# Leftover columns of a row transform as 32-row products with split frequency tables, and 64 small products ahead of the first column product

## Chip, cores, metric

The kernel runs on one core of one Trainium2 chip. The metric is the device time of one execution in microseconds. Three runs of the kernel before gave 494.93, 494.39 and 494.04 us, median 494.39 us.

## What is computed

```python
def _A_ref(x, w_r, w_i):                       # x: 1 x 2048 x 576
    X = rfft2(x.astype(float32), axes=(-2, -1))
    X = X * (w_r + 1j * w_i)
    return irfft2(X, s=(S, D)).astype(bfloat16)

def _B_ref(x, w_gate, w_up, w_down):           # 576 -> 4608 -> 576
    return (_gelu(x @ w_gate) * (x @ w_up)) @ w_down

h  = x + _A_ref(_layernorm(x), A_w_r, A_w_i)
h2 = h + _B_ref(_layernorm(h), B_w_gate, B_w_up, B_w_down)
```

x has 2048 rows of 576 values in bfloat16. The first part is a layer norm, a two-dimensional Fourier transform, a product with a filter and the transform back. The second part is a gated feed-forward network. The change lies in the forward transform.

## The kernel before, in words

The 2048 rows lie as 128 partitions by H = 16 (`h_sb`, partition p and index h hold row 16p + h). Every transform is a matrix product on TensorE with tables of sines and cosines that the kernel makes itself. The order on each engine is the order of the program text (a manual schedule); nothing is reordered between engines, and a wait on an engine holds all that is behind it on that engine.

The head of the kernel goes like this.

- **Statistics.** For most h VectorE takes mean and variance (`sd`, lines 379 to 387); for h = 1, 3, 5, 9, 11 ScalarE does (`ln_act`, line 128). GpSimd turns variances into reciprocal deviations (lines 137, 138), in the groups 0 to 3, 4 to 7, 8 to 11, 12 and 13, 14 and 15, and also issues two gathers of filter rows (line 397).
- **Tables.** ScalarE makes a table `fs` (line 218) by a sine, VectorE makes `F16` of it (`row_table`, line 298), and `small_table` (line 429) is the first use of it on TensorE. Then `fill` (line 316) gives TensorE 12 products of 512 columns whose result is not used.
- **First row step.** `norms` (line 389) scales `F16` by the reciprocal deviations into `FR` (line 391, VectorE), and `row16(h)` multiplies the 128-column blocks of row group h by it (lines 327 and 334, six products of 256, 256 and 128 columns for each half). 512 of the 576 columns are done so, in four blocks: columns 0 to 127 and 128 to 255, and the same from DH = 288 on.
- **Leftover columns.** Columns 256 to 287 and 544 to 575 are left. `row16_rest(h)` takes 64 columns from 256 and 64 from 512, so that 32 of each are needed and 32 overlap with what `row16` has; the two products write partitions 0 to 63 and 64 to 127 of one PSUM bank. Two more with `mneg` take the mean away. `rests(h)` does this for four h: 16 products of 128 columns with 64-column weights. It is called four times, after h = 3, 7, 11 and 15.
- **Evictions.** `evict` (line 361, ScalarE) copies two h at a time from PSUM into `Bt`; `evict4` (line 367) copies four h of leftovers, 128 x 512 values, on ScalarE for h = 0 and 4 and on VectorE for 8 and 12. All PSUM tiles come from one ring of four (`two`), so a new tile waits for the eviction of the fourth one before it.
- **Column step.** `f2(c)` (line 550) multiplies a 128-column slice of `Bt` by `DT` (four products of 290 columns) and `DF` (two, for the leftovers). `DF` is `D3` with the partitions of the overlapping columns set to zero. For the first c the two `DF` products stand last. `f2_out` (line 561) copies out on ScalarE. From here on the column products, the filter, the transform back and the feed-forward network follow, TensorE being busy nearly all the time.
- **Tables for the way back.** `load_dq` (line 518, DMAs on SyncE's queue) copies the rows of `DT` for frequencies into `DQ`; `iD` (lines 205 to 207) says which column each partition stands for.

Of the kernel before, what the change touches and what calls it, by code (L numbers as in the profile page):

```python
# [9 lines left out]
ACT = mybir.ActivationFunctionType  # L10
ALU = mybir.AluOpType
FP32 = mybir.dt.float32
BF16 = mybir.dt.bfloat16
# [7 lines left out]
P = 128  # L21
S = 2048
H = 16
D = 576
DH = D // 2
J = D // 2 + 1
JP = J + 1
JH = JP // 2
# [5 lines left out]
JW = 58  # L34
NW = JP // JW
# [7 lines left out]
def kernel_body(  # L43
# [11 lines left out]
    nc = tc.nc  # L55
    V = nc.vector
    A = nc.scalar
    G = nc.gpsimd
    T = nc.tensor

    ctx.enter_context(tc.manual_schedule())
    keep = ctx.enter_context(tc.tile_pool(name="keep", bufs=1))
# [4 lines left out]
    def two(name):  # L67
        return psum.tile([P, 2, 512], FP32, name=name, tag="two", bufs=4)

    h_sb = keep.tile([P, H, D], BF16, name="h_sb")  # L70
# [6 lines left out]
    def const(name, val):  # L77
        t = keep.tile([P, 1], FP32, name=name)
        V.memset(t[:], val)
        return t  # L80

    zerob = const("zerob", 0.0)
    pib = const("pib", PI)
    npib = const("npib", -PI)
    hpib = const("hpib", 0.5 * PI)
    nhpib = const("nhpib", -0.5 * PI)
# [5 lines left out]
    mneg = keep.tile([P, 2, H], BF16, name="mneg")  # L92
# [5 lines left out]
    Bt = keep.tile([P, NDT, S], BF16, name="Bt")  # L98
# [4 lines left out]
    ident = keep.tile([P, P], BF16, name="ident")  # L103
# [4 lines left out]

    DT = keep.tile([P, 3, 2, 2, JH], BF16, name="DT")
    D3 = DT[:, 2]  # L110
    DF = keep.tile([P, 2, 2, JH], BF16, name="DF")
    DQ = keep.tile([P, NW, 2, JH], BF16, name="DQ")
    mv = keep.tile([P, H, 2], FP32, name="mv")
    rstd = keep.tile([P, H], FP32, name="rstd")
# [67 lines left out]
    def tmp(name, shape, dtype=I32):  # L182
        return scr.tile(shape, dtype, name=name)

    def iota(t, pattern, base=0, cm=0):
        G.iota(t, pattern=pattern, base=base, channel_multiplier=cm, allow_small_or_imprecise_dtypes=True)

    V.memset(DF[:], 0.0)
    V.memset(DT[:, :, 1, :, JH - 1], 0.0)

    iu, ic = tmp("iu", [P, H, 8]), tmp("ic", [P, H, 8])
# [12 lines left out]
    make_identity(nc, ident[:])  # L204
    iD = tmp("iD", [P, 3], FP32)
    iota(iD[:], [[P, 3]], 0, 1)
    iota(iD[64:128, 2:3], [[0, 1]], 2 * P + 64 + 192, 1)
    iJ = tmp("iJ", [P, 2 * JM], FP32)
    iota(iJ[:], [[1, 2], [2, JM]])
    iDs = tmp("iDs", [P, 3], FP32)  # L210
# [72 lines left out]
    def minus_sine(sl):  # L283
        V.tensor_scalar(TF[:, sl, 0, :], TF[:, sl, 2, :], -1.0, None, op0=ALU.mult)
# [25 lines left out]
    ps_f = {}  # L310
# [28 lines left out]
                stop=True,  # L339
            )  # L340

    def rests(h):
        ps_f["f4", h] = two("f4")
        for i in range(4):
            row16_rest(h + i)

    def row16_rest(h):
        o = (h % 4) * P
        for mean in (False, True):
            for p0, d0 in ((0, 256), (64, 512)):  # L350
                T.matmul(
                    ps_f["f4", h - h % 4][p0 : p0 + 64, 0, o : o + P],
                    lhsT=mneg[:, 1, h : h + 1].to_broadcast([P, 64]) if mean else h_sb[:, h, d0 : d0 + 64],
                    rhs=FR[:, h, 0, :],
                    start=not mean,
                    stop=mean,
                )

    def evict(*hs):
        for h in hs:  # L360
            A.copy(  # L361
                Bt[:, 0:4, :].rearrange("p t (c h l) -> p (t c) h l", c=16, h=16)[:, :, h : h + 2, :],
                ps_f[h][:].rearrange("p h (tc l) -> p tc h l", l=8),
            )

    def evict4(h):
        (V.tensor_copy if h >= 8 else A.copy)(
            Bt[:, 4, :].rearrange("p (c h l) -> p h c l", c=16, h=16)[:, h : h + 4, :, :],
            ps_f["f4", h][:, 0].rearrange("p (h c l) -> p h c l", h=4, c=16),
        )  # L370

    agg = []
# [16 lines left out]
    def norms(lo, hi):  # L389
        for h in range(lo, hi):  # L390
            V.tensor_scalar(FR[:, h], F16[:], rstd[:, h : h + 1], None, op0=ALU.mult)  # L391
            row16(h)
# [12 lines left out]
    FR = fr_pool.__enter__().tile([P, H, 2, P], BF16, name="FR")  # L405
# [10 lines left out]
    def mirror(r):  # L416

        for a in range(2):
            dst, src, sg = DT[:, :, a, r, JM - a : JH - a], DT[:, :, a, r, JM - 2 :: -1], sgn[:, r : r + 1]
            V.tensor_scalar(dst, src, sg, None, op0=ALU.mult)  # L420
# [38 lines left out]
    minus_means(4, 8)  # L459
    gather(0)  # L460
    norms(0, 4)
    rests(0)
    minus_sine(first)
    turn_tf(first)
    sd(8, 10)
    flush()
    norms(4, 8)
    rests(4)
    ln_fin(slice(9, 12, 2))
    ln_rstd(rstd, mv, 8, 12)  # L470
    minus_means(8, 12)
    gather(1)
    evict(0, 2)
    evict4(0)
    evict(4, 6)
    evict4(4)
    sd(12, 13)
    flush()
    ln_rstd(rstd, mv, 12, 14)
    minus_means(12, 14)  # L480
    phases(0)
    norms(8, 12)
    rests(8)
    sd(14, 15)
    flush()
    ln_rstd(rstd, mv, 14, 16)
# [2 lines left out]
    phases(1, 2)  # L489
    drop_sign(kd[:], pd[:])  # L490
    norms(14, 16)
    rests(12)
    evict(8, 10)
    col_sin(1, pd, zerob)
    col_sin(0, kd, hpib)
    evict(12, 14)
    mirror(1)
    mirror(0)
    evict4(8)
    V.tensor_copy(DF[0:32], D3[0:32])  # L500
    V.tensor_copy(DF[96:128], D3[96:128])
    evict4(12)
    for w, t in ((WR, wm[0]), (WI, wm[1])):
        nc.sync.dma_start(w[:, 9 : H + 1, 0:J], t[:].rearrange("p (r j) -> p r j", r=8))
    angle_a(rest)
# [6 lines left out]
    def load_dq(r):  # L512
        for w in range(1 - r, NW):
            j0, j1 = w * JW, (w + 1) * JW
            for lo, hi in ((j0, min(j1, (j0 // P + 1) * P)), ((j0 // P + 1) * P, j1)):
                if lo < hi:
                    p0 = 64 * r + lo - j0
                    nc.sync.dma_start(
                        DQ[p0 : p0 + hi - lo, w], DT[lo % P : lo % P + hi - lo, lo // P, :, r, :]
                    )  # L520

    load_dq(1)

# [12 lines left out]
    order = [1, 2, 3, 4, 5, 6, 7, 0]  # L536
# [4 lines left out]
    slot = {k + 8 * e: 8 * x + 4 * e + i for k, (x, i) in place.items() for e in range(2)}  # L541

    def f2(c):
        ps = two("pq_ps")
        col = slice(slot[c] * P, (slot[c] + 1) * P)
        steps = [(par, t) for par in range(2) for t in (par, par + 2, 4)]
        if c == order[0]:
            steps.sort(key=lambda s: s[1] == 4)
        for par, t in steps:
            T.matmul(  # L550
                ps[:, par, 0:JP],
                lhsT=Bt[:, t, col],
                rhs=DT[:, t // 2, par] if t < 4 else DF[:, par],
                start=(t == par),
                stop=(t == 4),
            )
        pq[c] = wk.tile([P, 2, JP], BF16, name="pq", tag="pq", bufs=6)
        pq_ps[c] = ps
# [179 lines left out]
    n = len(order)  # L738
# [75 lines left out]
    def p_sb(f):  # L814
        if f >= NP0 and len(P_sb) == 1:
            P_sb.append(fp.tile([P, NFT - NP0, 4 * P], BF16, name="P_sb", tag="P1"))
        return P_sb[f // NP0][:, f % NP0, :]
# [138 lines left out]
    for h in range(4, H):  # L956
        b = 6 * (h // 2 - 2)
# [4 lines left out]
        b = h // 4 * NFT - NFT + 3 * (h % 4) + 2 + 16 * (h < 8)  # L962
# [36 lines left out]
    for tcnk in range(4):  # L999
        for gi in range(NG):  # L1000
# [7 lines left out]
            n = tcnk * NG + gi  # L1008
# [4 lines left out]
        for st in range(4):  # L1013
            h = tcnk * 4 + st
            if h < H - 1:
                accs = [two("acc") for _ in range(2)]
                for f in range(NFT):
                    for c in range(2):
                        for i in range(2):
# [3 lines left out]
                                lhsT=p_sb(f)[rows, st * P : (st + 1) * P],  # L1023
                                rhs=wd[f // NWA][rows, f % NWA, c * DH : (c + 1) * DH],
                                start=(f == 0),
                                stop=(f == NFT - 1),
# [9 lines left out]
            for c in range(2):  # L1036
                cc = slice(c * DH, (c + 1) * DH)
                acc = two("acc")
                for f in range(NFT):
                    T.matmul(  # L1040
                        acc[:, 0, 0:DH],
                        lhsT=p_sb(f)[:, st * P : (st + 1) * P],
                        rhs=wd[f // NWA][:, f % NWA, cc],
                        start=(f == 0),
                        stop=(f == NFT - 1),
# [54 lines left out]
```

## Time and profile before

| | us |
|---|---|
| median of three runs | 494.39 |
| the profiled execution, time | 494.6 |
| the profiled execution, span from first to last instruction | 492.8 |
| outside the span | 1.8 |
| TensorE busy in the span | 484.7 |
| first column product starts (after the span's start) | 21.96 |

The span is read from the left: the first 22 us are the head described above, 22 to about 65 us are the rest of the spectral part, and everything behind is the feed-forward network. All starts below are counted from the span's start. A busy TensorE is not TensorE at its peak: a product's recorded duration has a latency in it, and the distance between the starts of products tells more.

### The profile page before, as it was taken

To read this page: it belongs to the slowest core of one execution; us is meant where nothing else is said; L and a number is where in the kernel's file an instruction comes from. 1 tells how busy PE (TensorE), PEld (TensorE's weight loads), DVE (VectorE), ACT (ScalarE), POOL (GpSimd) and SP (SyncE) were. 2 spreads that over 40 slices of the span, in tenths; PEclk is the share of its full clock that TensorE was granted. 3 is DMA by queue.
4 is the path that set the end of the run, shared out by engine and by line. 5 is a ranking of instruction groups with operands and counts; after the bars stand their busy time and mean duration, and the time that the engine had idled before them with its cause. 6 is when DMAs were issued, how large, how long until landed. Compare 5 with 4: busy or idle time off the path is not lost.

```text
span 492.8 us, 12868 instructions
## 1 busy us (share of the span) xinstructions
PE 484.7 (98%) x5762; PEld 338.9 (69%) x5762; DVE 223.4 (45%) x457; ACT 158.2 (32%) x280; POOL 29.5 (6%) x84
## 2 busy tenths in 40 slices
PE   6999999999999999999999999999999999999997
PEld 3777789875589955555699755555799655555995
DVE  8999774798622177333311345333121333333111
ACT  8899863322210022332200132332110232232000
POOL 8500010011100011000000000000000000000000
PEclk9999999999999999999999999999999999999999
DMA  8838979769970049966720089876600377760000
GB/s 278 234 74 184 246 115 240 165 128 212 223 161 3 3 118 195 192 145 147 152 65 1 37 170 199 174 145 147 143 3 3 92 158 155 150 146 1 14 13 25
DMA packets 89582, 62.35 MB, mean 127 GB/s; under 512 B 23222, under 2 KB 88118, under 8 KB 89526
## 3 DMA queue, kind: packets, MB, share of 16 engines
q1 hardware_dynamic: 89238, 60.34, 57.5%
q0 software_dynamic: 288, 1.18, 0.7%
q8 instruction: 45, 0.74, 0.7%
q14 instruction: 11, 0.09, 0.1%
HBM read 52.65 MB, written 2.36 MB: 112 GB/s over the span
## 4 chain that ended last, share of the span: by engine, by line
PE 95%; ACT 2%; POOL 1%; DMA 1%; issue 0%; DVE 0%; ACTq 0%; POOLq 0%
PE gu L978 57%; PE acc L1021 27%; PE pq_ps L550 2%; PE cs_ps L709 2%; PE acc L1040 2%; PE eo_ps L658 2%; ACT junk L128 1%; PE y_ps L848 1%; PE gh_ps L568 1%; PE gh_ps L567 1%; DMA h_sb<-in_A_x_dram 1%; POOL rstd L138 1%; ACT Bt L361 0%; POOL wm_r L397 0%; PE eo_ps L682 0%
## 5 line engine op out<-in xcount | busy, mean ns | idle before, releaser
L978 PE MATMUL gu<-Bt,wgu 64*128 64x512 bf16 (+1 forms) x2646 | 270.6, 363 | 0.0
L978 PEld LDWEIGHTS <-wgu 64*128 64x128 bf16 x2646 | 151.5, 94 | 115.6 <-issue 0.3
L987 DVE TENSOR_TENSOR P_sb<-g_sb,gu 128x512 bf16<-128x512 f32 (+1 forms) x156 | 100.4, 645 | 140.3 <-ACT g_sb L986 140.3
L986 ACT ACTIVATE g_sb<-gu 128x512 f32<-128x512 f32 (+1 forms) x156 | 88.0, 564 | 193.5 <-PE gu L978 193.5
L1021 PEld LDWEIGHTS <-P_sb 64*128 64x128 bf16 x2160 | 122.2, 94 | 10.9
L1021 PE MATMUL acc<-wd,P_sb 64*128 64x288 bf16 x1440 | 90.9, 283 | 0.0
L1030 DVE TENSOR_TENSOR part<-part,acc 128x576 f32<-128x576 f32 x15 | 11.3, 754 | 112.6 <-ACT part L1029 112.6
L1029 ACT COPY part<-acc 128x576 f32<-128x576 f32 x15 | 9.6, 639 | 122.8 <-PE acc L1021 122.8
L1021 PE MATMUL acc<-wd_a,P_sb 64*128 64x288 bf16 x720 | 46.8, 283 | 0.0
L550 PE MATMUL pq_ps<-DT,Bt 128*128 128x290 bf16 x64 | 12.3, 286 | 0.7 <-ACT Bt L361 0.7
L978 PE MATMUL gu<-Bt,wgu_e 64*128 64x256 bf16 (+1 forms) x162 | 12.5, 305 | 0.0
L873 DVE TENSOR_SCALAR hrow<-h_sb,mv,rstd 128x1152 bf16<-128x1152 bf16 x14 | 12.2, 868 | 0.6 <-POOL rstd L911 0.6
L138 POOL TENSOR_TENSOR rstd<-rstd,mhalf 128x1 f32<-128x1 f32 (+2 forms) x17 | 12.0, 709 | 1.4
L1032 DVE TENSOR_TENSOR h_sb<-h_sb,part 128x576 bf16<-128x576 bf16 x15 | 11.4, 758 | 0.5
L550 PEld LDWEIGHTS <-Bt 128*128 128x128 bf16 x96 | 9.1, 97 | 3.4 <-ACT Bt L361 0.8
L978 PEld LDWEIGHTS <-wgu_e 64*128 64x128 bf16 x162 | 10.3, 94 | 1.2
L137 POOL TENSOR_SCALAR rstd<-mv 128x1 f32<-128x1 f32 (+2 forms) x17 | 4.1, 242 | 116.7 <-DVE mv L123 116.0
L561 ACT CAST pq<-pq_ps 128x580 bf16<-128x580 f32 x16 | 10.5, 666 | 1.2 <-PE pq_ps L550 1.1
L709 PE MATMUL cs_ps<-DQ,EO 58*128 58x290 bf16 x144 | 10.8, 283 | 0.0
L327 PE MATMUL f2t<-FR,h_sb 128*128 128x256 bf16 x64 | 9.2, 273 | 0.6 <-DVE FR L391 0.6
L709 PEld LDWEIGHTS <-EO 58*128 58x128 bf16 x160 | 7.8, 94 | 2.4 <-issue 0.7
L550 PE MATMUL pq_ps<-DF,Bt 128*128 128x290 bf16 x32 | 8.9, 285 | 0.0
(149 smaller groups left out, 283.9 us busy)
## 6 DMA issues: line engine op xcount, KB each, us to landing
wgu<-in_B_w_gate_dram SPq DMA_DIRECT2D x46, 432.0 KB, 5.1
wgu<-in_B_w_up_dram SPq DMA_DIRECT2D x46, 432.0 KB, 6.1
wd_a<-in_B_w_down_dram SPq DMA_DIRECT2D x1, 1728.0 KB
wd<-in_B_w_down_dram SPq DMA_DIRECT2D x1, 1728.0 KB
wd<-in_B_w_down_dram SPq DMA_DIRECT2D x6, 288.0 KB, 7.9
out_dram<-h_sb SPq DMA_DIRECT2D x3, 576.0 KB
h_sb<-in_A_x_dram SPq DMA_DIRECT2D x4, 288.0 KB, 4.3
h_sb<-in_A_x_dram SPq DMA_DIRECT2D x2, 576.0 KB
```

The source lines that it names most:

```text
L138: G.tensor_tensor(dst[:, sl], dst[:, sl], mhalf[:, sl], ALU.pow)
L550: T.matmul(ps[:, par, 0:JP], lhsT=Bt[:, t, col], rhs=DT[:, t // 2, par] if t < 4 else DF[:, par], start=(t == par), stop=(t == 4),)
L561: copy(pq[c][:, rs].rearrange("p r (j a) -> p r j a", a=2), pq_ps[c][:, :, 0:JP].rearrange("p a (r j) -> p r j a", r=2)[:, rs],)
L658: T.matmul(pv[:, n], lhsT=z[:, a, w].rearrange("p b j -> p (b j)"), rhs=TI[:, ts[k], 1 - a : 3 - a, :], start=(a == 0), stop=(a == 1),)
L709: T.matmul(ps[:, e, 0:JP], lhsT=EO[x][rows, w, 2 * g : 2 * g + 2].rearrange("p h e k l -> p (h e k l)"), rhs=DQ[rows, w] if w or e else DT ...
L873: V.tensor_scalar(hrow[:], h_sb[:, h, :].rearrange("p (r k) -> p r k", k=64).unsqueeze(2).to_broadcast([P, NR, 2, 64]), mv2[:, h, 0:1], rs ...
L978: T.matmul(gu[:, c, 0:n], lhsT=w[rows, r, i * P : (i + 1) * P], rhs=hl[tcnk % 2][rows, r, lo:hi], start=(r == 0), stop=(r == NR - 1),)
L986: A.activation(g_sb, gu[:, 0, 0:n], ACT.Gelu_apprx_tanh)
L987: V.tensor_tensor(p_sb(f)[:, lo:hi], g_sb, gu[:, 1, 0:n], ALU.mult)
L1021: T.matmul(accs[i][:, c, 0:DH], lhsT=p_sb(f)[rows, st * P : (st + 1) * P], rhs=wd[f // NWA][rows, f % NWA, c * DH : (c + 1) * DH], start=( ...
L1030: V.tensor_tensor(part, part, accs[1][:, :, 0:DH], ALU.add)
L1032: V.tensor_tensor(hv, hv, part, ALU.add)
```

## The change

- The leftovers of eight h go into one PSUM bank. For each h, both halves x of the 128 frequencies and both column groups n get a product of their own: weights of 32 columns, 64 moving columns, PSUM partitions 64x + 32n to 64x + 32n + 31. With the mean this makes 8 products for each h where there were 4, 64 for a call of `rests` where there were 16, and two calls (after h = 7 and h = 15) where there were four.
- So `evict4` runs twice, once on ScalarE (h = 0) and once on VectorE (h = 8), on 128 x 512 values each, and fills half of the columns of `Bt[:, 4]`.
- `f2` reads these columns by `slot % 8`, and `DF` gets a second version: one with the lower 64 partitions set, the other with the upper, zero elsewhere. The `DF` products stay two for each c.
- The zeros of `DF` are made in part by a VectorE memset of 64 partitions and in part by a ScalarE activation on the other 64; three more activations make `edge`, two rows of constants in the free half of `Bt[:, 4]`. All four activations stand ahead of that of `fs`.
- `iD` needs three `iota` on 32 partitions where there was one on 64.
- `load_dq` takes the last two rows of `DQ` from `edge`, one more DMA for each of its two calls.
- Ahead of the first column product 64 products of 16 columns with 32-column weights are put, into the PSUM tile that the column product then overwrites.

```diff
-    DF = keep.tile([P, 2, 2, JH], BF16, name="DF")
+    DF = keep.tile([P, 2, 2, 2, JH], BF16, name="DF")
+    edge = Bt[0:2, 4, 8 * P : 8 * P + 4 * JH].rearrange("p (r a j) -> p r a j", r=2, a=2)
...
-    V.memset(DF[:], 0.0)
+    V.memset(DF[64:128, 0], 0.0)
+    for t, b in (
+        (DF[0:64, 1].rearrange("p b a j -> p (b a j)"), zerob),
+        (edge[:, 0, 0], hpib),
+        (edge[:, 0, 1], nhpib),
+        (edge[:, 1].rearrange("p a j -> p (a j)"), zerob),
+    ):
+        n = t.shape[0]
+        A.activation(t, zerob[0:n].to_broadcast(list(t.shape)), ACT.Sin, bias=b[0:n])
...
-    iota(iD[64:128, 2:3], [[0, 1]], 2 * P + 64 + 192, 1)
+    for p0, d0 in ((32, 544), (64, 256), (96, 544)):
+        iota(iD[p0 : p0 + 32, 2:3], [[0, 1]], d0, 1)
...
-    def rests(h):
-        ps_f["f4", h] = two("f4")
-        for i in range(4):
-            row16_rest(h + i)
-
-    def row16_rest(h):
-        o = (h % 4) * P
-        for mean in (False, True):
-            for p0, d0 in ((0, 256), (64, 512)):
-                T.matmul(
-                    ps_f["f4", h - h % 4][p0 : p0 + 64, 0, o : o + P],
-                    lhsT=mneg[:, 1, h : h + 1].to_broadcast([P, 64]) if mean else h_sb[:, h, d0 : d0 + 64],
-                    rhs=FR[:, h, 0, :],
-                    start=not mean,
-                    stop=mean,
-                )
+    def rests(h0):
+        ps = ps_f["f4", h0] = two("f4")
+        for h in range(h0, h0 + 8):
+            o = (h - h0) * 64
+            for mean in (False, True):
+                for x in range(2):
+                    for n in range(2):
+                        p0, d0 = 64 * x + 32 * n, 256 + DH * n
+                        T.matmul(
+                            ps[p0 : p0 + 32, 0, o : o + 64],
+                            lhsT=mneg[:, 1, h : h + 1].to_broadcast([P, 32]) if mean else h_sb[:, h, d0 : d0 + 32],
+                            rhs=FR[:, h, 0, 64 * x : 64 * x + 64],
+                            start=not mean,
+                            stop=mean,
+                        )
...
     def evict4(h):
-        (V.tensor_copy if h >= 8 else A.copy)(
-            Bt[:, 4, :].rearrange("p (c h l) -> p h c l", c=16, h=16)[:, h : h + 4, :, :],
-            ps_f["f4", h][:, 0].rearrange("p (h c l) -> p h c l", h=4, c=16),
+        (V.tensor_copy if h else A.copy)(
+            Bt[:, 4, 0 : 8 * P].rearrange("p (c h l) -> p h c l", c=8, h=H)[:, h : h + 8],
+            ps_f["f4", h][:, 0].rearrange("p (h c l) -> p h c l", h=8, c=8),
         )
...
     norms(0, 4)
-    rests(0)
     minus_sine(first)
     turn_tf(first)
     sd(8, 10)
     flush()
     norms(4, 8)
-    rests(4)
+    rests(0)
...
-    evict(0, 2)
+    evict(0, 2, 4, 6)
     evict4(0)
-    evict(4, 6)
-    evict4(4)
...
     norms(8, 12)
-    rests(8)
...
     norms(14, 16)
-    rests(12)
+    rests(8)
...
+    for x in range(2):
+        V.tensor_copy(DF[64 * x : 64 * x + 64, x], D3[64 * x : 64 * x + 64])
     evict4(8)
-    V.tensor_copy(DF[0:32], D3[0:32])
-    V.tensor_copy(DF[96:128], D3[96:128])
-    evict4(12)
...
+        p0 = 64 * r + DH % JW
+        nc.sync.dma_start(DQ[p0 : p0 + 2, NW - 1], edge[:, r])
...
     def f2(c):
         ps = two("pq_ps")
         col = slice(slot[c] * P, (slot[c] + 1) * P)
+        col4 = slice(slot[c] % 8 * P, (slot[c] % 8 + 1) * P)
+        if c == order[0]:
+            for _ in range(64):
+                T.matmul(ps[0:32, 0, 0:16], lhsT=ident[:, 0:32], rhs=h_sb[:, 0, 0:16], start=True, stop=True)
...
-                lhsT=Bt[:, t, col],
-                rhs=DT[:, t // 2, par] if t < 4 else DF[:, par],
+                lhsT=Bt[:, t, col if t < 4 else col4],
+                rhs=DT[:, t // 2, par] if t < 4 else DF[:, slot[c] // 8, par],
```

More of the change, by code (lines that the diff above doesn't have):

```diff
@@ L514, in load_dq @@
             j0, j1 = w * JW, (w + 1) * JW
-            for lo, hi in ((j0, min(j1, (j0 // P + 1) * P)), ((j0 // P + 1) * P, j1)):
+            for lo, hi in ((j0, min(j1, (j0 // P + 1) * P)), ((j0 // P + 1) * P, min(j1, DH))):
                 if lo < hi:
```

## The prediction

> **What bounds the kernel now.** I read the page's first two parts, then the chain of waits, then the order of time for the first 25 us.
>
> ```profile
> PE 484.7 (98%) x5762; PEld 338.9 (69%) x5762; DVE 223.4 (45%) x457; ACT 158.2 (32%) x280; POOL 29.5 (6%) x84
> ...
> PE   6999999999999999999999999999999999999997
> ```
>
> TensorE is busy for 98% of the span, and the only slice with a real hole is the first (12.3 us each). So what is won or lost in the head is won or lost at the end, unless something behind it absorbs it. The chain of waits says who sets the head's length (start, duration, what):
>
> ```profile
> 8.85 2.78 ACT junk L128 x8
> ...
> 12.98 0.20 POOL sq L132
> ...
> 18.00 1.06 POOL rstd L138
> ...
> 19.10 0.30 DVE FR L391
> ...
> 19.43 0.67 ACT DT L408
> 20.10 1.82 ACT Bt L361 x2
> ...
> 21.96 2.46 PE pq_ps L550 x18
> ...
> 30.71 0.74 PE pq_ps L550 x6
> ```
>
> To 19.1 us it is statistics on GpSimd, then the last `FR`, then ScalarE's last two evictions; at 21.96 the first column product starts, and from there TensorE is the chain. The second column is what matters in the last row: six column products take 0.74 us.
>
> Does anything behind 22 us absorb a late start? Busy time by engine, 22 to 34 us, and the wait that holds ScalarE there:
>
> ```profile
> 22.00:34.00 12.00, 11.93 (x94) 8.88 (x95) 11.86 (x24) 10.76 (x19) 1.29 (x7) 1.00 0.36 89
> ```
>
> ```profile
> ACT pq L561 <- PE pq_ps L550: 1.1, 1, 1.1
> ```
>
> TensorE is idle for 0.07 of 12 us. ScalarE is idle for 1.24, of which 1.1 is one wait, for the first column product. So a later start of that product moves both full engines by as much, and I take the delay to the end one for one.
>
> **The change, part by part.** Times are those of the profiled execution (494.6 us: span 492.8, 1.8 around it).
>
> *1. Four sines ahead of `fs`, on ScalarE.* The rows at the beginning:
>
> ```profile
> 0.72 1.28 ACT L218 ACT_TABLE_LOAD   x1 [0.72 <-PEq L1084]
> ...
> 2.81 0.40 ACT L218 ACTIVATE fs<-mu,npib 128x128 f32<-128x128 int32 x1 [0.80 <-DVE mu L216]
> ...
> 3.36 0.28 DVE L298 SCALAR_TENSOR_TENSOR F<-iu,fs 128x128 bf16<-128x128 int32 x1
> ...
> 3.70 0.68 ACT L128 ACTIVATE junk<-h_sb 128x576 bf16<-128x576 bf16 x1 [0.48 <-DMA h_sb<-in_A_x_dram]
> ...
> 4.05 5.14 PE L316 MATMUL f2t<-h_sb,ident 128*128 128x512 bf16 x12
> ...
> 5.98 0.46 DVE L384 BATCH_NORM_STATS2 st<-h_sb 128x6 f32<-128x288 bf16 x1 [0.52 <-DMA h_sb<-in_A_x_dram]
> ...
> 7.71 0.49 ACT L278 ACTIVATE TF<-pr,pib 128x256 bf16<-128x256 int32 x1
> ...
> 8.11 0.49 ACT L281 ACTIVATE TF<-ab,nhpib 128x256 bf16<-128x256 f32 x1
> ...
> 9.35 0.21 DVE L377 BATCH_NORM_AGGREGATE mv<-st 128x2 f32<-128x12 f32 x1
> 9.47 0.82 DVE L391 TENSOR_SCALAR FR<-F,rstd 128x256 bf16<-128x256 bf16 x4
> 9.72 0.27 POOL L137 TENSOR_SCALAR rstd<-mv 128x4 f32<-128x4 f32 x1 [0.48 <-DVE FR L391]
> 9.76 0.38 PE L327 MATMUL f2t<-FR,h_sb 128*128 128x256 bf16 x2 [0.57 <-DVE FR L391]
> ```
>
> ```profile
> 24.34 1.04 ACT L278 ACTIVATE TF<-pr,pib 128x896 bf16<-128x896 int32 x1
> ```
>
> A sine of 256 values takes 0.49 us and one of 896 takes 1.04, so 0.86 ns a value and 0.27 fixed; the next starts 0.09 before the end (7.71 to 8.11). The four have 580, 145, 145 and 290 values (fewer partitions change nothing that I can see): 0.68 + 0.30 + 0.30 + 0.43 = 1.7 us. The table load ends at 2.00, so `fs` starts at 3.7 instead of 2.81 and the statistics on ScalarE at 4.03 instead of 3.70. That 0.33 is hidden: ScalarE's last statistics end at 11.63 (8.85 + 2.78), and GpSimd first reads them at 12.98, behind a gather. `F` goes from 3.36 to about 4.2 and holds VectorE, which is behind it, by 0.75; the 0.52 that VectorE waits for x before 5.98 swallow most, and **0.2 us** stay. VectorE is then busy without a hole to 9.35, and the GpSimd row at 9.72 waits for that result, so its whole chain of reciprocal deviations, and the last `FR`, come 0.2 later (19.3). The fill products start 0.85 later and end near 10.0 instead of 9.2; row group 0 starts about 0.25 late, which is hidden by the `FR` of group 4, below. The memset keeps its 580 values for each partition, and the two extra `iota` (0.3 on GpSimd) end before the wait at 9.72. I take 0.2, with bounds of 0 and 0.35.
>
> *2. `rests` moved and made of 32-row products.* Order of time around them:
>
> ```profile
> 14.91 0.25 PE L351 MATMUL f<-FR,h_sb 128*64 128x128 bf16 x2
> ...
> 15.48 0.39 PE L327 MATMUL f2t<-FR,h_sb 128*128 128x256 bf16 x2
> ...
> 17.05 1.93 ACT L361 CAST Bt<-f2t 128x1024 bf16<-128x1024 f32 x2
> ...
> 19.10 0.48 DVE L391 TENSOR_SCALAR FR<-F,rstd 128x256 bf16<-128x256 bf16 x2
> ...
> 19.45 0.38 PE L327 MATMUL f2t<-FR,h_sb 128*128 128x256 bf16 x2
> ...
> 20.50 0.22 PE L334 MATMUL f2t<-FR,mneg 128*128 128x128 bf16 x1
> 20.64 0.25 PE L351 MATMUL f<-FR,h_sb 128*64 128x128 bf16 x2
> 20.73 0.22 PE L351 MATMUL f<-FR,mneg 128*64 128x128 bf16 x2
> ...
> 21.06 0.22 PE L351 MATMUL f<-FR,mneg 128*64 128x128 bf16 x2
> ...
> 21.96 0.67 PE L550 MATMUL pq_ps<-DT,Bt 128*128 128x290 bf16 x4 [0.68 <-ACT Bt L361]
> 22.52 0.42 PE L550 MATMUL pq_ps<-DF,Bt 128*128 128x290 bf16 x2
> ```
>
> ```profile
> L351 PE MATMUL f<-FR,h_sb x32: 219/219/243, 12.0 to 21.0; 128*64 128x128 bf16 x32
> ```
>
> Two products of 64-column weights together cover 0.22 us while each alone takes 0.219: they run side by side, on different columns of the array, and a pair follows a pair every 0.055 (20.73 to 21.06, six steps). Weights and moving columns are now both half as wide, and four products fill the array, so I take a group of four at half of that, 0.028; 64 products are 16 groups, 0.45, as the 16 products (8 pairs) took before. The first call stands behind row group 7, where one stood anyway (14.91), so group 8 starts as before. The call between 11 and 12 goes, but that time isn't won: the last `FR` (19.10, now 19.3) releases group 14, and 9.47 to 9.76 says that a product starts 0.29 after `FR` does. Group 14 starts at 19.6 instead of 19.45, **0.15 late**, and the last `rests` at 20.79, ending at 21.27.
>
> *3. Evictions.* The rows of `evict4`:
>
> ```profile
> L367 ACT CAST Bt<-f x2: 586/586/587, 13.3 to 16.6; 128x512 bf16<-128x512 f32 x2
> L367 DVE CAST Bt<-f x2: 677/684/691, 20.5 to 21.8; 128x512 bf16<-128x512 f32 x2
> ```
>
> One on ScalarE (0.59 us) and one on VectorE (0.68) go; the two that stay copy as many values each. ScalarE's gain is hidden behind the same late groups 14 and 15: the last `evict` ends at about 22.07 (21.92 + 0.15). VectorE's remaining `evict4` follows `rests` and ends near 22.2; both are done before TensorE asks for them, below.
>
> *4. The 64 small products.* All write the same 32 columns of the array, so none runs beside another. Nothing in the trace is as small. Nearest row: the 0.055 from one product to the next on the same 64 columns. Halving it with the weights' width gives 0.028; scaling it with the moving columns alone (16 of 128) gives 0.007, the lower end; not scaling it gives 0.055, the upper. I take 0.028, because a load of weights precedes every product and its work goes with the weights' width: 64 x 0.028 = **1.8 us**. They wait for a PSUM tile that ScalarE has emptied by 19 us (17.05 + 1.93), so they run from 21.27 to 23.05. Leaving narrow weights costs 0.09 (20.50 to 20.64, less the 0.055 of the product itself). So the first column product starts at 23.14, **1.18 later** than 21.96. TensorE had 0.68 idle there that the small products fill, and they take 1.1 more than that.
>
> The Trainium skill, "TensorE: Matmul & The Clock Gate", section "Back-to-back issue gap", gives about 25 ns from start to start for any product of 1 to 64 columns. By that the 64 would be 1.6 us and the sum 0.2 less, an estimate from that page; no row here has such a product.
>
> *5. The first column.* Before, its four `DT` products took 0.56 (21.96 to 22.52) where 0.74 x 4 / 6 = 0.49 was needed, since `DF` waited for VectorE. That 0.07 goes. Later `f2` have the same products. The DMAs of `edge` lengthen SyncE's queue by one each, far ahead of the use of `DQ`; I cost them at nothing, and at under 1 us if a weight load behind them were late.
>
> Sum: + 0.15 + 1.03 (the rest of the 1.18) - 0.07 = **+1.1 us**: 495.7 against 494.6. The median lies 0.2 under the profiled execution, so 495.5.
>
> **Rivals.**
>
> *Small products nearly free.* At 0.007 they end at 21.72; the column product then waits for the last eviction as before, at 22.11, and the sum is + 0.15 - 0.07 = 0.1: **494.5**, no change. It decides below 0.012 each, (22.11 - 0.09 - 21.27) / 64. For it: an order in which small products exactly fill a hole of 0.7 us. Against: the weights' load.
>
> *Small products at 0.055.* Another 1.8 us: **497.3**. For it: the only measured distance on one set of columns. Against: that distance also fits the 128 moving columns, eight times as many.
>
> *Narrow products one by one.* If a product can't start within 0.028 of the last, whatever its columns, `rests` takes 64 x 0.028 = 1.8 us. Group 8 then starts at 16.8, group 14 at 20.1, the last `rests` runs 21.3 to 23.1, the small ones to 24.85, the column product starts at 24.94: + 2.9, **497.3**. For it: 0.055 for a pair is also 0.028 a product. Against: both of a pair start together. The floor of 25 ns named above would be this rival, were it one for the whole array; the pairs' rows speak against that.
>
> *The clock falls.* The fill's 12 products took 5.14 us, 0.43 each for 512 columns; a pair of 128 columns took 0.055 later, so TensorE was at about half speed before it warmed. If 2.3 us of narrow work count as rest, the narrow stretch and a few microseconds behind run at half speed: + 3 to 5, about **498.5**. For it: narrow products light a quarter of the array. Against: nothing like it at the four `rests` before.
>
> *Faster.* At most the 0.68 us of idle time could go, which isn't 0.2% of 494 us; it would need something that I don't see.
>
> **How the numbers follow.** Forecast 0.58, own range 495.0 to 496.1 (the 0 to 0.35 of part 1, 0.025 to 0.035 for each small product). Nearly free 0.17, one by one 0.09, at 0.055 each 0.05, clock 0.04, faster 0.07. The range takes in both ends of the small product's cost: 494.2 to 497.4. About 0.2%, 1 us, is what a measurement of this kernel can tell from no change: a quarter of the forecast's chance lies under it. Slower: 0.44 + 0.09 + 0.05 + 0.04 = 0.62; same: 0.14 + 0.17 = 0.31; faster: 0.07.
>
> **What would show it.** The first of the 64 products near 21.3 and the first column product near 23.1; 64 narrow products of a `rests` in about 0.45 us; ScalarE's first statistics at 4.03; the last `FR` at 19.3; no idle time on TensorE between row group 15 and the column products. It is wrong if the column product starts before 22.5, if `rests` takes over 1 us, or if the 22 to 34 us stretch shows a hole that takes the delay up.

## The result, and the profile after

The changed kernel takes 495.57 us (median of 14 runs, 495.44 to 495.95), the kernel before 494.63 us beside it (median of 14, 494.04 to 494.93). The ratio is 1.0021, with a 95% interval of 1.0012 to 1.0029: slower by about 1 us, as forecast (495.5). The profiled execution after took 495.46 us against 494.6, 0.86 more; that difference is what the rows have to explain.

ScalarE's first rows after (start, duration, what) show the four sines ahead of `fs`:

```profile
2.02 0.78 ACT L197 ACTIVATE DF<-zerob 64x580 bf16<-64x580 f32 x1
...
3.73 0.38 ACT L228 ACTIVATE fs<-mu,npib 128x128 f32<-128x128 int32 x1
4.03 0.67 ACT L129 ACTIVATE junk<-h_sb 128x576 bf16<-128x576 bf16 x1
```

`fs` at 3.73 and the statistics at 4.03 are where they were forecast. VectorE's rows tell how much of that arrives at the last `FR`:

```profile
4.15 0.37 DVE L308 SCALAR_TENSOR_TENSOR F<-iu,fs 128x128 bf16<-128x128 int32 x1 [0.70 <-ACT fs L228]
...
6.09 0.44 DVE L393 BATCH_NORM_STATS2 st<-h_sb 128x6 f32<-128x288 bf16 x1
...
19.17 0.48 DVE L400 TENSOR_SCALAR FR<-F,rstd 128x256 bf16<-128x256 bf16 x2
```

`F` comes 0.79 later than before, the row that stood at 5.98 behind a wait of 0.52 stands at 6.09, and the last `FR` is 0.07 late (19.17 against 19.10).

TensorE at the end of the head: the last of 16 rows of four narrow products, then the small ones, then the first column product.

```profile
20.71 0.21 PE L360 MATMUL f<-FR,h_sb 128*32 128x64 bf16 x4
...
21.18 0.22 PE L360 MATMUL f<-FR,mneg 128*32 128x64 bf16 x4
21.21 1.75 PE L555 MATMUL pq_ps<-h_sb,ident 128*32 128x16 bf16 x64
22.90 0.67 PE L560 MATMUL pq_ps<-DT,Bt 128*128 128x290 bf16 x4
23.41 0.41 PE L560 MATMUL pq_ps<-DF,Bt 128*128 128x290 bf16 x2
```

No row has a wait: from 20.71 on TensorE always has something. The column product starts at 22.90, 0.94 later than before; its `DT` products follow each other without the old wait for `DF` (0.51 to the `DF` row, before 0.56). 0.94 - 0.05 is 0.89, the 0.86 of the result. Behind that nothing gives it back: the same stretch as before has TensorE busy all the time, and ScalarE's wait for the first column product grew by 0.2.

```profile
22.00:34.00 12.00, 12.00 (x128) 9.45 (x125) 11.37 (x22) 10.56 (x18) 1.20 (x7) 1.00 0.32 78
```

```profile
ACT pq L571 <- PE pq_ps L560: 1.3, 1, 1.3
```

So far this is the forecast. But one place in the same execution was in no part of it. TensorE's rows behind the first call of `rests`:

```profile
15.24 0.22 PE L360 MATMUL f<-FR,mneg 128*32 128x64 bf16 x4
15.46 0.27 PE L337 MATMUL f2t<-FR,h_sb 128*128 128x256 bf16 x1
15.91 0.27 PE L337 MATMUL f2t<-FR,h_sb 128*128 128x256 bf16 x1 [0.18 <-issue]
...
16.07 0.27 PE L337 MATMUL f2t<-FR,h_sb 128*128 128x256 bf16 x1
16.61 0.27 PE L337 MATMUL f2t<-FR,h_sb 128*128 128x256 bf16 x1 [0.27 <-issue]
```

Two products of a pair normally start 0.11 apart; here the second comes 0.45 and 0.54 after the first (15.46 to 15.91, 16.07 to 16.61). That is some 0.77 us lost, and the releaser is "issue": TensorE waited for nothing that the profile shows. I call this the pause. The second call, the same 64 products at 20.71 to 21.21, has none behind it: the first small product follows at 21.21. ScalarE, which copies out these row groups, hands it on:

```profile
16.88 0.58 ACT L376 CAST Bt<-f 128x512 bf16<-128x512 f32 x1 [0.98 <-PE f L360]
...
20.64 1.91 ACT L370 CAST Bt<-f2t 128x1024 bf16<-128x1024 f32 x2
```

Its last two evictions end at 22.55, where the forecast had 22.07. The column product reads what they write. So two things are late at once: the small products, behind which the column product starts at 22.90, and the evictions, which end at 22.55. The profile can't say what one would cost without the other.

### The profile page after: what moved, and what is told of

Same layout as the page of the kernel before. It is cut to its first block, busy times and chain, and to the rows that moved or that the text cites. A ratio compares the mean times of both kernels' runs of the same rounds, so it can differ in the third digit from the quotient of the medians.

```text
span 493.7 us, 13130 instructions
## 1 busy us (share of the span) xinstructions
PE 484.4 (98%) x5890; PEld 340.1 (69%) x5890; DVE 222.8 (45%) x456; ACT 159.1 (32%) x283; POOL 29.3 (6%) x86
## 3 DMA queue, kind: packets, MB, share of 16 engines
q0 software_dynamic: 288, 1.18, 0.8%
## 4 chain that ended last, share of the span: by engine, by line
PE 97%; DVE 2%; ACT 1%; issue 0%
PE gu L988 57%; PE acc L1031 27%; PE pq_ps L560 2%; PE cs_ps L719 2%; PE acc L1050 2%; PE eo_ps L668 2%; PE f2t L337 1%; PE y_ps L858 1%; PE gh_ps L578 1%; PE gh_ps L577 1%; DVE st L393 1%; DVE st L395 0%; PE pq_ps L555 0%; PE f2t L344 0%; ACT L197 0%; PE eo_ps L692 0%
```

## The experiments

The first theory is the prediction's: the small products, 25 to 28 ns each, put the column product off by what they take beyond TensorE's old idle time, and nothing else matters. The rival: the pause behind the burst of narrow products (the first call of `rests`) makes ScalarE late, and would cost most of the 1 us with no small product at all. Each group below ran on one chip, the groups on different ones; that turned out to matter.

### The small products alone, and all but them

The kernel before with the 64 small products:

```diff
     def f2(c):
         ps = two("pq_ps")
         col = slice(slot[c] * P, (slot[c] + 1) * P)
+        if c == order[0]:
+            for _ in range(64):
+                T.matmul(ps[0:32, 0, 0:16], lhsT=ident[:, 0:32], rhs=h_sb[:, 0, 0:16], start=True, stop=True)
```

> The kernel before with nothing but the 64 small products added ahead of the first column product (in the changed kernel 64 of them take 1.69 us with the step back to wide weights). In the kernel before the last narrow product starts at 21.06 and the column product at 21.96, so they should fill 0.8 us of idle time and cost 0.8: first column product at about 22.8, + 0.8 us. That is the size that both theories give for the products themselves; the theory that they are nearly free gives under + 0.1.

Measured: 495.17 us against 494.43, ratio 1.0012 (1.0002 to 1.0022). The profiled execution was the slowest of its 13 (497.49 us) and isn't used for the sum. It shows something else, in a row of TensorE and in one stretch (busy times by engine, then the granted clock, third from the right):

```profile
10.23 0.46 PE L327 MATMUL f2t<-FR,h_sb 128*128 128x256 bf16 x2 [1.98 <-DVE FR L391]
```

```profile
10.40:13.81 3.41, 3.41 (x22) 2.57 (x21) 3.38 (x15) 2.29 (x5) 3.01 (x6) 0.50 1.33 265
```

In that one execution TensorE waited 1.98 us for the first `FR`, and right behind it its clock fell to half for 3.41 us, long before the first small product (23.34).

The changed kernel without the small products:

```diff
-        if c == order[0]:
-            for _ in range(64):
-                T.matmul(ps[0:32, 0, 0:16], lhsT=ident[:, 0:32], rhs=h_sb[:, 0, 0:16], start=True, stop=True)
```

> The changed kernel without the 64 small products. Theory 1 (the prediction's): they alone make the column product late; without them it waits for the last eviction on ScalarE, which should end near 22.0: first column product at 22.0 to 22.1, 0.85 us less than the changed kernel, + 0.1 against before. Theory 2 (from the trace): TensorE's pause at 15.5 to 16.6 us, behind the first call of rests, makes ScalarE's evictions 0.66 late whatever stands ahead of the column product; the last ends at 22.55, the column product starts at 22.6, only 0.3 less than the changed kernel, + 0.6 against before. Third: if the small products are there to hold the clock, it falls here and the time rises by over 1 us.

Measured: 494.54 us against 494.43, ratio 1.0001 (0.9991 to 1.0011). Its rows, TensorE's first and then ScalarE's:

```profile
15.46 0.38 PE L337 MATMUL f2t<-FR,h_sb 128*128 128x256 bf16 x2
...
21.89 0.67 PE L557 MATMUL pq_ps<-DT,Bt 128*128 128x290 bf16 x4 [0.48 <-ACT Bt L370]
```

```profile
19.88 1.96 ACT L370 CAST Bt<-f2t 128x1024 bf16<-128x1024 f32 x2
```

No pause, evictions done at 21.84, the column product at 21.89. Here the first theory holds whole: without the small products the change costs nothing that can be measured, and in the kernel before they alone cost 0.7 us.

### The width of the weights, and more instructions ahead

Three kernels with the 64 small products in place. The first gives them 64-column weights:

```diff
-                T.matmul(ps[0:32, 0, 0:16], lhsT=ident[:, 0:32], rhs=h_sb[:, 0, 0:16], start=True, stop=True)
+                T.matmul(ps[0:64, 0, 0:16], lhsT=ident[:, 0:64], rhs=h_sb[:, 0, 0:16], start=True, stop=True)
```

> The changed kernel, the 64 small products with weights of 64 columns instead of 32, still 16 moving columns. By the prediction's step 4 the cost goes with the weights' width: 0.055 each, 3.5 us, the column product at 24.8, + 1.9 us against the changed kernel. If there is a least distance of 25 ns between products whatever the weights: 1.6 us, no difference.

Measured: 496.02 us against 494.43, ratio 1.003 (1.0019 to 1.0041). The second, on the same chip, keeps the small products and makes the fill of 48 products of 128 columns, so that 36 more products stand ahead of the first burst:

```diff
-        for _ in range(n):
-            T.matmul(dst, lhsT=ident[:], rhs=h_sb[:, 0, 0:512], start=True, stop=True)
+        for i in range(4 * n):
+            q = slice(i % 4 * P, i % 4 * P + P)
+            T.matmul(dst[:, q], lhsT=ident[:], rhs=h_sb[:, 0, q], start=True, stop=True)
```

> The changed kernel with the 12 fill products of 512 columns cut into 48 of 128: same work, 72 more instructions on TensorE ahead of the row products. If the pause behind the first call of rests comes from running out of instructions at a certain number of them, it starts 72 instructions earlier, about 36 products, so inside the 64 narrow products, near the 28th. If it comes from going from narrow to wide weights, it stays where it is, in row group 8 behind the last narrow product. Little change of the time by either.

Measured in one run: 495.57 us. The third, on another chip, gives the small products all 128 columns of weights:

```diff
-                T.matmul(ps[0:32, 0, 0:16], lhsT=ident[:, 0:32], rhs=h_sb[:, 0, 0:16], start=True, stop=True)
+                T.matmul(ps[:, 0, 0:16], lhsT=ident[:], rhs=h_sb[:, 0, 0:16], start=True, stop=True)
```

> The changed kernel, the 64 small products with weights of 128 columns, 16 moving columns. With 32 columns they were 25 ns apart, with 64 columns 32 ns. If the distance grows with the weights' width, 45 to 65 ns, and the column product starts at 24 to 25.4; if only narrow weights are loaded slowly, 25 to 32 ns, and it starts at 22.8 to 23.3, without the step back to wide weights.

Measured in one run: 495.81 us. The rows of the small products and of the column product, of the kernels with 64 columns, with the other fill, and with 128 columns:

```profile
21.34 2.19 PE L555 MATMUL pq_ps<-h_sb,ident 128*64 128x16 bf16 x64
23.46 0.67 PE L560 MATMUL pq_ps<-DT,Bt 128*128 128x290 bf16 x4
```

```profile
21.34 1.75 PE L556 MATMUL pq_ps<-h_sb,ident 128*32 128x16 bf16 x64
23.03 0.67 PE L561 MATMUL pq_ps<-DT,Bt 128*128 128x290 bf16 x4
```

```profile
21.66 1.76 PE L555 MATMUL pq_ps<-h_sb,ident 128*128 128x16 bf16 x64
23.27 0.66 PE L560 MATMUL pq_ps<-DT,Bt 128*128 128x290 bf16 x4
```

From the first small product to the column product: 2.12, 1.69 and 1.61 us, with the step to wide weights in it. From the first small product to the last (the row's length less the 0.17 that one lasts, by 63) they follow each other every 32, 25 and 25 ns. The time doesn't follow the weights' width, which the prediction scaled it by: 128 columns cost no more than 32, and only 64 cost more. The 0.43 us between the first two came out in the time (496.02 against the one run of 495.57): a delay here reaches the end one for one, as forecast. The first two had no pause, the third had it. The one with the other fill took 495.57, as much as the changed kernel, whose profile has the pause; a delay by the pause that the small products cover is not seen in the time.

### Fewer, faster and more small products

On the second chip. First 16 instead of 64:

```diff
-            for _ in range(64):
+            for _ in range(16):
```

> The changed kernel with 16 small products instead of 64. They take 0.4 us from 21.2, end at 21.6 and, with 0.09 for the step to wide weights, are done before the last eviction at 21.84: free, column product at 21.9, 494.55 us as without any. If small products cost something of themselves beyond their time, more than that.

Measured: 495.35 us against 494.28, ratio 1.002 (1.001 to 1.0029). Then 64 dealt over the four column groups of the array:

```diff
-            for _ in range(64):
-                T.matmul(ps[0:32, 0, 0:16], lhsT=ident[:, 0:32], rhs=h_sb[:, 0, 0:16], start=True, stop=True)
+            for i in range(64):
+                T.matmul(ps[32 * (i % 4) : 32 * (i % 4) + 32, 0, 0:16], lhsT=ident[:, 0:32], rhs=h_sb[:, 0, 0:16], start=True, stop=True)
```

> The changed kernel, the 64 small products dealt in turn to the four groups of 32 columns of the array, as the products of rests are. Prediction's step 4: they are slow because they share one group of columns; dealt over four, 16 groups of four follow each other every 0.03, 0.5 us, and end at 21.7, before the last eviction: the column product starts at 21.9 as without any small products, 494.55 us. If there is a least distance of 25 ns between any two products, whatever their columns, nothing changes: 22.9, 495.55 us.

Measured: 495.26 us against 494.28, ratio 1.0021 (1.0012 to 1.0031). By the first theory both should have been level with the kernel before, and neither was. The first theory falls as the whole story. TensorE's rows of the kernel with 16:

```profile
15.79 0.27 PE L337 MATMUL f2t<-FR,h_sb 128*128 128x256 bf16 x1
16.24 0.28 PE L337 MATMUL f2t<-FR,h_sb 128*128 128x256 bf16 x1 [0.18 <-issue]
...
16.95 0.27 PE L337 MATMUL f2t<-FR,h_sb 128*128 128x256 bf16 x1 [0.26 <-issue]
...
21.54 0.55 PE L555 MATMUL pq_ps<-h_sb,ident 128*32 128x16 bf16 x16
22.95 0.67 PE L560 MATMUL pq_ps<-DT,Bt 128*128 128x290 bf16 x4 [0.85 <-ACT Bt L370]
```

The small products are done after 0.4 us, and TensorE then waits 0.85 us for ScalarE's eviction. The pause is there and sets the end by itself. The kernel with the dealt products has it too:

```profile
16.11 0.27 PE L337 MATMUL f2t<-FR,h_sb 128*128 128x256 bf16 x1
16.58 0.28 PE L337 MATMUL f2t<-FR,h_sb 128*128 128x256 bf16 x1 [0.20 <-issue]
...
21.91 0.84 PE L555 MATMUL pq_ps<-h_sb,ident 128*32 128x16 bf16 x64
23.32 0.67 PE L560 MATMUL pq_ps<-DT,Bt 128*128 128x290 bf16 x4 [0.56 <-ACT Bt L370]
```

In this execution the whole head came about 0.65 later, and so did the pause (16.11 against 15.46): it belongs to its place in the program and not to a moment. Dealt over four column groups, the 64 take some 0.65 us from the first start to the last (0.84 less the 0.18 that one product lasts): 10 ns each.

Last, 128 of them:

```diff
-            for _ in range(64):
+            for _ in range(128):
```

> The changed kernel with 128 small products instead of 64. If each is 25 ns and all of it is on the path: the column product at 24.5, + 1.6 us against the changed kernel, 497.2 us. If something else made the column product late, less than that.

Measured: 499.76 us against 494.28, ratio 1.0106 (1.0078 to 1.0133), 4.2 us above the changed kernel's 495.57 where 1.6 was expected. Three of its four runs (499.41 to 500.49) have a mean granted clock of 0.996 or 0.997; the fourth, 497.76, has 1.000. The stretches of one of the three, and then TensorE's rows:

```profile
21.24:24.87 3.63, 2.90 (x133) 2.80 (x120) 3.48 (x6) 1.24 (x2) 0.78 (x4) 1.00 0.68 192
24.87:28.28 3.41, 3.32 (x30) 2.29 (x31) 0.90 (x2) 0.64 (x1) 0.42 (x3) 0.50 0.22 49
```

```profile
21.24 2.90 PE L555 MATMUL pq_ps<-h_sb,ident 128*32 128x16 bf16 x110
24.96 0.65 PE L555 MATMUL pq_ps<-h_sb,ident 128*32 128x16 bf16 x18 [0.82 <-issue]
```

This is the rival of the falling clock, at twice the change's number: the clock is at half for 3.41 us, and the first column products run at half speed (four take 1.15 us instead of 0.67). A second pause by "issue", 0.82 us, stands between the 110th and the 111th small product. In this execution the pause came first: it begins at 24.14 (21.24 + 2.90), and the clock falls at 24.87. Whether the products alone would lower the clock isn't shown.

### The same kernels again on a third chip

The kernel without small products, that with 16, and that with 16 and the fill of 48, together. The edits are those above.

> The changed kernel without the 64 small products, once more, beside the kernel with 16 of them on the same chip. Theory A (the pause of TensorE behind the first narrow products comes with the chip or the program's load, whatever stands at the first column product): if the kernel with 16 has the pause here, this one has it too, its last eviction ends near 22.5 and its time is about 495.2; if neither has it, both are near 494.5. Theory B (the pause belongs to the kernel, by where its instructions lie): no pause here, column product at 21.9, 494.5, while the kernel with 16 has it again. The time is read rightly only beside that one.

Measured: 495.41 us against 494.37, ratio 1.0015 (1.0003 to 1.0027). The same program had given 494.54 on the first chip; all 10 runs here (495.07 to 495.96) lie above 11 of its 12 there.

> 16 small products instead of 64, once more, beside the kernel with none. Their own 0.4 us fit into the 0.6 us for which TensorE waits for ScalarE, so without the pause the column product starts near 21.95 and the time is 494.5. Theory A: the pause comes and goes with the chip or load, so this kernel and the one without small products have it together or lack it together. Theory B: it is in this kernel always: pause, column product near 22.6 to 22.9, 495.2 to 495.4, while the one with none stays at 494.5.

Measured: 495.4 us, ratio 1.0018 (1.0008 to 1.0028).

> 16 small products, and the fill as 48 products of 128 columns instead of 12 of 512, so that 36 more matmuls and their weight loads run ahead of the first narrow products for the same work. If the pause is TensorE running out of loaded instructions (it does at the point where some 265 had run), the stock is asked for about 72 instructions sooner, in the slow part of the head where there is time to load: no pause of 0.2 us or over behind the first narrow products, column product near 22.0, and 494.4 to 494.7, against 495.2 to 495.4 for the kernel with 16 and the old fill if that one has the pause. If the pause has another cause, both kernels are alike within 0.3 us.

Measured: 495.31 us, ratio 1.0016 (1.0007 to 1.0026). TensorE in the kernel without small products:

```profile
15.52 0.27 PE L337 MATMUL f2t<-FR,h_sb 128*128 128x256 bf16 x1
16.00 0.27 PE L337 MATMUL f2t<-FR,h_sb 128*128 128x256 bf16 x1 [0.21 <-issue]
...
16.73 0.38 PE L337 MATMUL f2t<-FR,h_sb 128*128 128x256 bf16 x2 [0.40 <-issue]
...
22.83 0.67 PE L557 MATMUL pq_ps<-DT,Bt 128*128 128x290 bf16 x4 [1.21 <-ACT Bt L370]
```

Theory A holds and B falls: for one and the same program the pause comes and goes, with the chip or with the load of the program on it; these runs don't tell the two apart. All three kernels have it here, and so had all four on the second chip; on the first, none of the three with this burst. With this the four cases stand beside each other, from three occasions:

| | no pause | pause |
|---|---|---|
| no small products | column product 21.89, 494.54 us | 22.83, 495.41 us |
| 64 small products | 23.03, 495.57 us (fill of 48, one run) | 22.90, 495.57 us (the changed kernel) |

Either cause alone makes up nearly the whole loss, and both together cost no more than one: the column product starts when the later of the two is done. (In the kernel with the fill of 48 the small products start at 21.34, 0.13 later than in the changed kernel; why isn't shown.) (The head of the execution at 22.83 was itself 0.2 late: the fill took 5.30 us there and 4.46 on the first chip, and row group 0 stood at 10.03, on the first chip at 9.85. So the pause alone is worth 0.7 to 0.9.)

The kernel with 36 more products ahead of the burst has the pause at the same place, right behind it (here 0.26 ahead of the first `mneg` row, then 0.56):

```profile
15.46 0.38 PE L338 MATMUL f2t<-FR,h_sb 128*128 128x256 bf16 x2
15.94 0.22 PE L345 MATMUL f2t<-FR,mneg 128*128 128x128 bf16 x1
15.99 0.27 PE L338 MATMUL f2t<-FR,h_sb 128*128 128x256 bf16 x1
16.66 0.28 PE L338 MATMUL f2t<-FR,h_sb 128*128 128x256 bf16 x1 [0.40 <-issue]
```

So it doesn't come after a certain count of instructions. That expectation missed: more instructions ahead of the burst don't take it away. In the kernel with 16 and the old fill it begins a little sooner, inside the burst, whose last row of four starts 0.66 behind the row before it:

```profile
15.25 0.22 PE L360 MATMUL f<-FR,h_sb 128*32 128x64 bf16 x4
15.91 0.24 PE L360 MATMUL f<-FR,mneg 128*32 128x64 bf16 x4 [0.44 <-issue]
```

### The burst cut in four

What is left is the burst itself: 64 products with 64 weight loads in 0.5 us. No small products, and the first call of `rests` in four parts of 16 products, one behind every second row group:

```diff
-    def rests(h0):
-        ps = ps_f["f4", h0] = two("f4")
-        for h in range(h0, h0 + 8):
+    def rests(h0, lo=0, hi=8):
+        if lo == 0:
+            ps_f["f4", h0] = two("f4")
+        ps = ps_f["f4", h0]
+        for h in range(h0 + lo, h0 + hi):
...
-    norms(0, 4)
+    for h in (0, 2):
+        norms(h, h + 2)
+        rests(0, h, h + 2)
...
-    norms(4, 8)
-    rests(0)
+    for h in (4, 6):
+        norms(h, h + 2)
+        rests(0, h, h + 2)
```

> No small products, and the first 64 narrow products in four bursts of 16 (32 TensorE instructions each, as many as a call had before the change), one behind every second row group. So far every execution on three occasions showed TensorE pausing some 0.7 us right behind the burst of 64 (128 instructions in 0.5 us) and every one on a fourth showed none, the same kernel without small products among both (495.4 and 494.5). If TensorE runs out of instructions because the burst takes them faster than they are brought, short bursts leave time to bring them: no pause on any chip, last eviction ends near 21.9, 494.5. If the pause belongs to the chip and to about that point of the program and not to the burst, it is here too where the chip has it: last eviction near 22.5, 495.3 to 495.4. On a chip that has no pause with the whole burst either, 494.5 would tell nothing; the time of the kernel before (494.3 to 494.4 on all so far) doesn't tell the chips apart.

Measured, on a fourth chip: 494.85 us against 494.58, ratio 0.9998 (0.9983 to 1.0013). No pause in its profile:

```profile
15.86 0.20 PE L362 MATMUL f<-FR,mneg 128*32 128x64 bf16 x4
15.99 0.39 PE L337 MATMUL f2t<-FR,h_sb 128*128 128x256 bf16 x2
16.22 0.22 PE L344 MATMUL f2t<-FR,mneg 128*128 128x128 bf16 x1
```

That fits a TensorE that is short of instructions behind a fast burst, and short bursts would be the cure. But no kernel with the whole burst ran on this chip, so it isn't shown: it may be a chip without the pause. Its execution, the slowest of the ten (495.16), was late from the start (row group 0 at 10.19), and 494.85 is 0.3 above the kernel without small products on the first chip. No version was seen to beat the kernel before.

## Why the prediction was right, point by point

The forecast of 495.5 us came true with 495.57, and the sequence that it gave for the changed kernel is the one in the profile. It left one cause out, the pause; the small products hid what that costs. How near the number came is in part luck: the kernel before took 494.63 beside it where the forecast started from 494.4, and the difference was 0.94 where it had 1.1, so the two nearly cancel.

1. **The sines.** `fs` at 3.73, the statistics at 4.03, `F` at 4.15: as worked out. Of 0.2 us at the last `FR` 0.07 was there (19.17). The wait of 0.52 ahead of 5.98 swallowed a little more than its length: the row there starts 0.91 behind the one ahead of it before (5.07 to 5.98) and 0.33 after (5.76 to 6.09), so the slack was 0.58, and the rows ahead of it took 0.1 less. The fill, forecast to end near 10.0, ended at 9.20 as before: it took 4.26 us where the forecast kept the 5.14, so row group 0 was 0.08 late (9.84) and not 0.25. The wait for the `FR` of group 4 (0.30 at 12.49) hides either.
2. **`rests`.** A row of four every 0.03 us (20.71 to 21.21, 16 rows, 0.50; forecast 0.45), so products in different columns run side by side at a quarter of the array too. The rival "narrow products one by one" (1.8 us) is out. The call ended at 21.21 instead of 21.27. What the step missed is what comes behind the first call: in this profile and in those of two of the chips a pause of 0.7 us, where the forecast had group 8 starting "as before".
3. **Evictions.** "The last `evict` ends at about 22.07" failed in the profiled execution: 22.55, because of the pause. In the kernel without small products on the first chip it was 21.84. VectorE's `evict4` ended at 22.65 (21.96 + 0.69, a row of VectorE's order of time) instead of 22.2, since the mirrored tables wait 0.57 for ScalarE's `DT`, which the pause made late; without the pause, on the first chip, it ended at 22.17. The small products hide both.
4. **The small products.** 25 ns each instead of 28: 21.21 to 22.90 is 1.69, of which 0.09 is the step to wide weights. (The forecast read its 0.09 from the step into narrow weights, 20.50 to 20.64; the step out of them came out the same.) The number was near, the reason given for it was not: it scaled the 0.055 by the weights' width, and 128 columns took the same 25 ns as 32. The column product came 0.94 late instead of 1.18. The Trainium skill, "TensorE: Matmul & The Clock Gate", section "Back-to-back issue gap", gives about 25 ns for any product of 1 to 64 columns. These rows agree with it for weights of 32 and of 128 columns; with weights of 64 it was more, 32 ns, and products dealt over the four column groups (10 ns) and those of `rests` (four in 0.03) were closer, so here it is a floor of one set of columns and not of the array.
5. **The first column.** 0.05 of the forecast 0.07 came back, and the delay reached the end one for one: 0.94 - 0.05 against 0.86.

**The rivals.** "Small products nearly free" was tried by 16 and by dealt products: 495.3 to 495.4 us on chips with the pause, not 494.5; without the pause and the products it is 494.54. What the rival lacked is the second cause, and its price is wrong too: 25 ns is above the 0.012 at which it decides. "At 0.055 each" is out. "The clock falls" is not what the change does (1.00 from 22 to 34 us); it fell in three of four runs of the kernel with 128, where in the profile a pause of 0.82 us stands ahead of it.

**What is shown and what stays open.** That the small products are enough for the loss is shown on the first chip (494.54 without, 495.57 with them and the longer fill in one run, 495.17 against 494.43 in the kernel before); the changed kernel itself was not run there. That the pause is enough is shown on the third (495.41 without them against 494.37). That it isn't fixed by the program is shown by one program on two chips; whether the chip or the load decides is open. That it stands at the burst's place is shown by the late head and by the longer fill. Why TensorE stops there is open: the profile says only "issue", the second burst of the same size has no pause behind it, an instruction transfer of the same size (0.02 MB) stands in the executions with and without the pause near that time, and the cut burst ran on a chip where the whole one was not tried.

## What to carry to other kernels

Two late things that end at the same point hide each other: taking one away shows little until the other is gone too, so an edit that gives no gain may still have removed a real cause, and a table of both, with and without, is the way to see it. An experiment whose effect is under a microsecond should be beside its control on the same chip: here the same program differed by 0.9 us between two occasions on different chips while the kernel before stayed within 0.4 (494.28 to 494.63). A product of 16 columns isn't a 16th of one of 256, which takes 0.11 us here: behind another on the same columns it takes 25 ns, so 64 of them fill 1.6 us. Without small products and without the pause 0.68 us lay free ahead of the column product (21.21 to 21.89); less the 0.09 of the step, an estimated 24 of them fill that.

## What the runs showed of the hardware

- TensorE can pause for some 0.7 us by "issue" at the end of 128 instructions (64 loads of weights, 64 products) taken in 0.5 us: in all seven profiles of two chips, and in none of three of another. A second burst of the same kind in the same execution had no pause behind it (21.18 to 21.21).
- Small products on the same columns follow each other every 25 ns with weights of 32 or 128 columns, every 32 ns with weights of 64; dealt over four column groups every 10 ns.
- Behind 2.90 us of such products and a pause of 0.82 (24.14 to 24.96) the granted clock was 0.50 for 3.41 us (24.87 to 28.28); the same length, 3.41 us at 0.50 (10.40 to 13.81), stands behind a wait of 1.98 us in that one execution of the kernel before with small products.
